# Transposing q and k by the DMA crossbar instead of TensorE in a linear-attention and MLP kernel

## The chip, the cores and the metric

The kernel runs on one core of a Trainium2 chip. The metric is the device time of one execution in microseconds (us). "Before" took 228.87 us as the median of three runs (227.82 to 230.3) when the prediction was written. The profile shows one such execution, whose span of instructions was 227.0 us. TensorE (PE) had its full clock throughout (0.999).

## The reference, cut to what matters

There are two parts. The first is causal linear attention with a decay for each head, in blocks, over q, k and v of shape (4, 8, 768, 64). Its output, as 3072 rows of 512 columns, goes through a two-layer MLP of width 2048 with a smooth ReLU.

```python
for b in range(nb):                                   # blocks of the sequence
    intra = einsum('bhic,bhjc->bhij', qb, kb) * Dmask # scores
    intra = einsum('bhij,bhjd->bhid', intra, vb)
    inter = einsum('bhid,bhde->bhie', qb * lam_pow, kv_state)
    out[:, :, sl] = intra + inter
    kv_state = lam_block * kv_state + einsum('bhsd,bhse->bhde', kb_dec, vb)
h = x @ w_in
g = where(h >= 1, h, where(h <= -1, 0, (h + 1) ** 2 / 4))
out = g @ w_out
```

## The kernel before: the parts that matter

The rows are cut into 24 chunks of 128 (`NCH`). The scores need q and k with the head dimension on the partitions, so each chunk's k and q (both 128 x 512) are transposed: first cast to bf16 by ScalarE, then transposed by eight TensorE instructions into PSUM (the memory that TensorE's results go to here), then copied or scaled from there by VectorE into SBUF (the on-chip memory that holds the other tiles).

```python
def f_t(c):                                           # TensorE
    ptt[c] = pp_t.tile([128, 2, HP, 128], BF16, name="pt", tag="pt")
    for i, x in ((1, ks), (0, qs)):
        for hp in range(HP):                          # HP = 4
            nc.tensor.transpose(out=ptt[c][:, i, hp, :], in_=pair(x[c], hp), identity=ident)

def f_kb(c, hi):                                      # VectorE: k, block-diagonal
    ...
        nc.vector.tensor_copy(kbd[c % NKB][HD[hi], :, :, hi, :], ptt[c][HD[hi], 1].rearrange(...))

def f_qT(c):                                          # VectorE: q times the decay table
    nc.vector.tensor_tensor(qT[c], ptt[c][:, 0], tab_q[:, c % NCB], op=AX.mult)

def f_vb(c, g, hi):                                   # v, block-diagonal, by DMA; VP = 12
    (nc.gpsimd if c < VP else nc.sync).dma_start(out=o, in_=i)
```

The MLP's first layer (`f_l1`, PSUM tile `ph`), its activation (r on ScalarE; t, w and gT on VectorE) and its second layer (`f_l2`, PSUM tile `py`) run between the attention's pieces.

The order of instructions on each engine is fixed when the kernel is built. A small planner in the kernel (`run_plan`) has a booked duration, a landing time and a due time for each operation, plays them through, and writes each engine's program in the order that it found. `STEP` spaces the due times. Each engine then works through its program in that order, so a wrong booked time can cost real time.

## Time and profile before

| engine | busy before | what it does |
|---|---|---|
| PE | 96% of the span | the MLP, the scores, the transposes |
| VectorE (DVE) | 70% | t, w, gT; kbd, qT and masks of the attention |
| ScalarE (ACT) | 60% | r, the casts, copies out of PSUM |
| GpSimd (POOL) | 33% | scaling of v, issue of some DMAs |

A share of busy time says little about what an engine's work is worth. That is read from the chain of waits (what ended last, followed back) and from the busy time of single stretches. The prediction below quotes those lines. One more is from the view of waits of the kernel before, with columns of total us, number of waits and the longest:

```profile
ACT r L347 <- DVE w L357: 9.7, 8, 1.2
```

ScalarE waits for VectorE's w step, because w is what frees the buffers that r is written to.

### The profile page before, as it was taken

What the parts mean: (1) busy time and instruction counts of PE and PEld (TensorE: products, weight loads), DVE (VectorE), ACT (ScalarE), POOL (GpSimd) and SP (SyncE); (2) the same over time, 40 slices, a digit from 0 to 9 for tenths busy, and PEclk for the clock granted to TensorE, in tenths of its full rate; (3) what the DMA queues carried; (4) which work ended last, traced back from release to release, by engine and by line L of the source; (5) the groups of instructions that cost most, each with busy time, mean ns of one, the idle gap of its engine ahead of it and who ended that gap; (6) DMA issues with size and microseconds to landing.
All of it is one profiled execution on the core that took longest, in us unless ns stands there. A gap on an engine that the chain in (4) does not pass through costs nothing.

```text
span 227.0 us, 5657 instructions
## 1 busy us (share of the span) xinstructions
PE 217.0 (96%) x2272; PEld 158.7 (70%) x2308; DVE 159.5 (70%) x276; ACT 136.6 (60%) x249; POOL 74.0 (33%) x95
## 2 busy tenths in 40 slices
PE   7799999989999999999999999999999999999993
PEld 2467888867787778877877777776777776766441
DVE  6635889998689998996678687783875775544300
ACT  6768575844988667588547648645565554545121
POOL 8999765956899420221032210000000000000000
PEclk9999999999999999999999999999999999999999
DMA  5999998969999999497687732112101101110212
GB/s 147 232 255 212 268 204 220 201 144 275 269 253 272 243 271 238 76 241 155 163 194 149 198 88 70 37 35 69 48 3 46 49 0 49 48 46 3 92 46 92
DMA packets 78570, 32.36 MB, mean 143 GB/s; under 512 B 69648, under 2 KB 73744, under 8 KB 78544
## 3 DMA queue, kind: packets, MB, share of 16 engines
q1 hardware_dynamic: 71632, 21.77, 38.8%
q0 software_dynamic: 6768, 10.23, 20.5%
q8 instruction: 18, 0.29, 0.5%
q14 instruction: 8, 0.07, 0.1%
q10 hardware_dynamic: 144, 0.00, 0.0%
HBM read 27.27 MB, written 6.29 MB: 148 GB/s over the span
## 4 chain that ended last, share of the span: by engine, by line
PE 78%; DVE 12%; POOL 4%; DMA 3%; issue 1%; ACT 0%; POOLq 0%; ACTq 0%
PE ph L339 32%; PE py L378 32%; PE pt L267 4%; DVE gT L372 3%; DMA w_in_sb<-in_moe_w_in_dram 3%; PE ps L298 3%; DVE t L353 3%; PE po L322 2%; DVE w L357 2%; PE po L316 2%; PE pu L286 2%; DVE sc L309 1%; POOL x2f L420 1%; DVE kbd L273 1%; POOL vn L254 1%
## 5 line engine op out<-in xcount | busy, mean ns | idle before, releaser
L347 ACT ACTIVATE r<-ph,one 128x512 bf16<-128x512 f32 x96 | 65.8, 687 | 60.5 <-PE ph L339 42.2
L339 PE MATMUL ph<-xT,w_in_sb 128*128 128x128 bf16 (+1 forms) x1152 | 98.9, 237 | 0.2 <-DMA w_in_sb<-in_moe_w_in_dram 0.2
L339 PEld LDWEIGHTS <-w_in_sb 128*128 128x128 bf16 x1152 | 81.7, 98 | 15.5 <-DMA w_in_sb<-in_moe_w_in_dram 0.4
L378 PE MATMUL py<-w_out_sb,gT 128*128 128x512 bf16 x351 | 89.8, 379 | 1.7
L378 PEld LDWEIGHTS <-gT 128*128 128x128 bf16 x384 | 34.6, 98 | 27.5
L254 POOL TENSOR_TENSOR vn<-x2f,tab_k 128x512 bf16<-128x512 f32 x24 | 27.6, 1151 | 52.2 <-DMA vi<-vn 22.7
L353 DVE TENSOR_SCALAR t<-r 128x1024 bf16<-128x1024 bf16 x48 | 25.3, 526 | 23.8 <-ACT r L347 23.7
L372 DVE TENSOR_TENSOR gT<-w,t 128x1024 bf16<-128x1024 bf16 x48 | 37.3, 778 | 1.1
L357 DVE TENSOR_TENSOR w<-r,t 128x1024 bf16<-128x1024 bf16 x48 | 35.4, 738 | 1.4
L309 DVE TENSOR_TENSOR sc<-ps,causal 128x512 bf16<-128x512 f32 (+1 forms) x40 | 22.1, 553 | 7.4 <-PE ps L298 7.4
L383 ACT COPY osb<-py 128x512 f32<-128x512 f32 x24 | 14.0, 585 | 15.7 <-PE py L378 15.2
L273 DVE COPY kbd<-pt 64x512 bf16<-64x512 bf16 x40 | 16.8, 419 | 7.1 <-PE pt L267 6.7
L261 POOL DMA_DIRECT2D vi<-vn x32 | 20.2, 647 | 2.7 <-POOL vn L254 2.4
L280 DVE TENSOR_TENSOR qT<-pt,tab_q 128x512 bf16<-128x512 bf16 x24 | 16.6, 690 | 1.7 <-ACT kbd L271 1.1
L329 ACT CAST xT<-po 128x512 bf16<-128x512 f32 x24 | 14.0, 583 | 5.6 <-PE po L322 4.1
L290 ACT CAST ubd<-pu 64x256 bf16<-64x256 f32 x40 | 14.6, 365 | 2.4 <-PE pu L286 2.1
L248 ACT CAST qs<-x0f 128x512 bf16<-128x512 f32 x23 | 14.2, 618 | 0.7 <-DMA x0f<-in_q_dram 0.7
L298 PE MATMUL ps<-qT,kbd 128*128 128x128 bf16 (+1 forms) x160 | 13.3, 206 | 1.4 <-DVE qT L280 0.8
L248 ACT CAST ks<-x1f 128x512 bf16<-128x512 f32 x23 | 14.2, 616 | 0.1
L316 PE MATMUL po<-qT,ubd 128*128 128x128 bf16 x80 | 13.8, 221 | 0.0
L298 PEld LDWEIGHTS <-kbd 128*128 128x128 bf16 x160 | 10.5, 98 | 4.4 <-issue 1.5
L322 PE MATMUL po<-sc,vi 128*128 128x128 bf16 (+1 forms) x160 | 13.2, 206 | 0.1
(50 smaller groups left out, 136.2 us busy)
## 6 DMA issues: line engine op xcount, KB each, us to landing
out_dram<-osb SPq DMA_DIRECT2D x24, 256.0 KB, 2.0
x1f<-in_k_dram SPq DMA_DIRECT2D x18, 256.0 KB, 4.1
x0f<-in_q_dram SPq DMA_DIRECT2D x18, 256.0 KB, 4.3
x2f<-in_v_dram SPq DMA_DIRECT2D x17, 256.0 KB, 4.1
w_in_sb<-in_moe_w_in_dram POOLq DMA_DIRECT2D x4, 512.0 KB, 7.5
w_out_sb<-in_moe_w_out_dram POOLq DMA_DIRECT2D x4, 512.0 KB, 9.8
x2f<-in_v_dram POOLq DMA_DIRECT2D x7, 256.0 KB, 4.7
x1f<-in_k_dram POOLq DMA_DIRECT2D x6, 256.0 KB, 6.6
```

Of the source, the lines that this page charges most:

```text
L248: nc.scalar.copy(out=t, in_=qkv_ld[c, x])
L254: nc.gpsimd.tensor_tensor(vn[c % NV].rearrange("p a b d -> p (a b) d"), qkv_ld[c, 2], _bc(tab_k[:, c % NCB, :], 2, D), op=AX.mult)
L261: (nc.gpsimd if c < VP else nc.sync).dma_start(out=o, in_=i)
L273: nc.vector.tensor_copy(kbd[c % NKB][HD[hi], :, :, hi, :], ptt[c][HD[hi], 1].rearrange("p a (b d) -> p a b d", b=2))
L298: nc.tensor.matmul(pst[c, g][:, hp, :], lhsT=kbd[c % NKB][:, hp, g].rearrange("p a d -> p (a d)"), rhs=qT[c][:, hp, 64 * g:], start=True, ...
L309: nc.vector.tensor_tensor(sc_sb[c][g], pst[c, g], _bc(causal[:, 0:128 - 64 * g], 1, HP), op=AX.mult)
L339: nc.tensor.matmul(ph[:, j * m:(j + 1) * m], lhsT=w_in_sb[:, ko, (i + j) * 128:(i + j + 1) * 128], rhs=xT[s][:, ko, p * m:(p + 1) * m], st ...
L347: nc.scalar.activation(out=r_t[grp][:, i, :], in_=ph_t[s, ni, part], func=AF.Relu, bias=one[:, 0:1])
L353: nc.vector.tensor_scalar(t_t[grp], r_t[grp], 0.5, 1.0, op0=AX.mult, op1=AX.min)
L357: nc.vector.tensor_tensor(w_t[grp], r_t[grp], t_t[grp], op=AX.subtract)
L372: nc.vector.tensor_tensor(o, w, t, op=AX.mult)
L378: nc.tensor.matmul(py_t[s, ms], lhsT=gT[s][:, ko, ms * 128:(ms + 1) * 128], rhs=w_out_sb[:, ko, :], start=(ko == 0), stop=(ko == FO - 1))
```

## The change

The intent is to take 128 transposes (16 chunks of eight) off TensorE. Chunks 8 to 23 are transposed by the DMA crossbar (a DMA that transposes while it copies), SBUF to SBUF, in one instruction for q and k together. It is issued by SyncE (SP), which here only issues DMAs. The other edits make room for it: q and k share one tile with four buffers, the v copies of chunks 12 to 23 move from SP to GpSimd, loads are released 30 us ahead of need, due times are spaced closer, and some of the planner's booked times change (left out below).

```diff
+    NQK, NXT, XT = 4, 2, 8
+    qkp = ctx.enter_context(tc.tile_pool(name="qkp", bufs=NQK))
+    xtp = ctx.enter_context(tc.tile_pool(name="xtp", bufs=NXT))
...
+    def f_xt(c):
+        t = xtp.tile([128, 2, HP, 128], BF16, name="xq", tag="xq")
+        ptt[c] = t
+        nc.sync.dma_start_transpose(out=t.rearrange("p a h k -> p (a h) k"), in_=qk[c].rearrange("p a h d -> p (a h d)"))
...
-    VP = 12
+    VP = 24
...
-                    rel = u.own - AHEAD if u.key[0] == "t" and u.key[1] >= CPS else 0
+                    rel = o_due(u.key[1]) - (14000 if u.key[0] == "t" else 18000) if u.key[0] in ("t", "xt") and u.key[1] >= CPS else o_due(u.key[1]) - 30000 if u.key[0] == "li" and u.key[1] > SW else 0
...
-    T0, STEP, LEAD = 24000, 1047, 3000
+    T0, STEP, LEAD = 24000, 1015, 3000
...
+        if c < XT:
+            add(t, "PE", mm(*[128] * 8), lambda c=c: f_t(c), need, due=od - 9000, extra=FILL)
+        else:
+            add(t, "SP", 2000, lambda c=c: f_xt(c), need, due=-0.7, extra=4500)
```

`f_kb` and `f_qT` are the same instructions as before, but for these chunks they read the transposed data from SBUF (xq) and no longer from PSUM (pt).

## The prediction

> **What bounds the kernel now.** I read the page's first part and its chain first, then the busy time in stretches, then the chain in order of time in two of them, and last the groups that the change touches.
>
> ```profile
> PE 217.0 (96%) x2272; PEld 158.7 (70%) x2308; DVE 159.5 (70%) x276; ACT 136.6 (60%) x249; POOL 74.0 (33%) x95
> ...
> PE 78%; DVE 12%; POOL 4%; DMA 3%; issue 1%; ACT 0%; POOLq 0%; ACTq 0%
> ```
>
> TensorE (PE) is busy for 96% of the span and holds 78% of the chain of waits. VectorE (DVE) holds 12% of the chain, so somewhere it is the bound for a while. A share over the whole span hides where, so next come the stretches; their columns are the stretch, its length, then busy time of PE, PEld, DVE, ACT and POOL.
>
> ```profile
> 60.00:80.00 20.00, 19.47 (x276) 16.13 (x279) 19.08 (x28) 16.05 (x33) 15.37 (x20) 1.00 1.09 256
> 80.00:100.00 20.00, 19.49 (x266) 15.69 (x268) 18.82 (x35) 14.23 (x26) 4.04 (x3) 1.00 0.87 204
> 120.00:140.00 20.00, 19.84 (x180) 14.54 (x183) 15.24 (x28) 13.21 (x26) 3.50 (x3) 1.00 0.53 129
> 160.00:180.00 20.00, 19.84 (x184) 14.45 (x184) 14.33 (x28) 12.34 (x21) 0.00 (x0) 1.00 0.11 41
> ```
>
> From 100 us on PE is busy for 19.8 of 20 us, VectorE for about 14, and the DMA engines have little to do (0.53 of their time, then 0.11). Between 60 and 100 us VectorE is nearly full too, and GpSimd (POOL) is busy for 15.4 of 20 us at first. A busy PE may still be a PE that runs with gaps, so I look at the chain in order of time in the late stretch; the columns are start, length, and what.
>
> ```profile
> 158.26 0.86 PE py L378 x4
> 159.13 0.87 PE ph L339 x8
> 160.00 0.45 PE pt L267 x8
> 160.45 0.86 PE py L378 x4
> 161.31 0.87 PE ph L339 x8
> 162.18 0.05 issue
> 162.24 0.81 PE py L378 x3
> ```
>
> Each piece starts where the one before ends; in the part from 156 to 178 us "issue", the only piece that isn't matmul work, is 0.7%. So the eight transposes of a chunk, four of k and four of q, cost the full 0.45 us of their issue there: PE work removed is time removed, as long as nothing takes its place. The other kind of stretch reads like this:
>
> ```profile
> 67.83 0.69 DVE sc L309
> 68.52 1.98 DVE t L353
> ...
> 75.42 0.61 DVE w L357
> 76.05 1.42 DVE gT L372
> ```
>
> From 67.8 to 85 us the chain runs on VectorE without a break, and the t step, whose shortest record is 408 ns, takes 1.98 us here. Last, the groups concerned:
>
> ```profile
> L267 PE MATMUL pt<-ident,ks 128*128 128x128 bf16 x96 | 9.3, 219 | 0.0
> L273 DVE COPY kbd<-pt 64x512 bf16<-64x512 bf16 x40 | 16.8, 419 | 7.1 <-PE pt L267 6.7
> L280 DVE TENSOR_TENSOR qT<-pt,tab_q 128x512 bf16<-128x512 bf16 x24 | 16.6, 690 | 1.7 <-ACT kbd L271 1.1
> L353 DVE TENSOR_SCALAR t<-r x48: 408/426/2051, 20.6 to 210.2; 128x1024 bf16<-128x1024 bf16 x48
> L261 SPq DMA_DIRECT2D vi<-vn x48: 590/597/1339, 89.0 to 156.3; - x48
> ```
>
> The first line's busy 9.3 us is not the cost to count: its 219 ns overlap with each other, and eight transposes advance the chain by 0.45 us, 56 ns each.
>
> **What the Trainium skill says.** (1) "VectorE: DVE Perf Modes", The perf-mode tier table: a copy from bf16 SBUF may run 4x, one with a PSUM operand at most 2x; a tensor_tensor with an fp32 operand stays 1x. The trace agrees on the ends it shows: 128x1024 bf16 SBUF to SBUF in 408 ns, the PSUM copy of 512 columns in 419 ns. (2) "SBUF — State Buffer", Who interferes with whom: VectorE in a two-port mode and GpSimd take an exclusive lock on a shared port pair, and a VectorE instruction with two SBUF inputs contends with a GpSimd instruction that reads SBUF. The trace agrees: t goes from 408 to 2051 ns, and averages 1.03 us (4.14 us for 4) in the stretch from 60 to 80 us where GpSimd is busy for 77%. (3) "DMA: Bandwidth & Descriptors", Latency and other measured facts, gives an effective 261 GB/s for a DMA transpose, and its part on the DMA transpose says that it must be issued from SP or ACT and must land in SBUF; no run here shows its speed yet. (4) "Advanced Engine Details and Errata", X-Bar Transpose (TRN2): transposes on two queues at once corrupt each other; here all sixteen are issued from SP, so no extra wait is needed.
>
> **The change, part by part.**
>
> PE work removed. Chunks 8 to 23 are 16 of 24, so 16 x 0.45 = 7.2 us of PE issue go. The stretches put the transposes of chunks 8 to 10 between 60 and 80 us; in the chain I count 14 of the 16 at full length, and two (chunks 9 and 10) fall in the VectorE stretch from 67.8 to 85 us. So 14 x 0.45 = 6.3 us are on the path that sets the end, and 0.9 us lie beside VectorE work.
>
> VectorE work removed. The 32 kbd copies of these chunks now read bf16 from SBUF. An estimate from the t step: it has 1024 columns in 408 ns; 512 columns fewer at four per cycle of 0.96 GHz (that page's clock) are 133 ns less, so 275 ns against 419, and the diff's own plan has 260. That is 0.15 x 32 = 4.8 us less VectorE work, of which some 0.6 us lies in the VectorE stretch (four copies). The qT multiply has an fp32 table as its second operand, so it stays at 690 ns.
>
> VectorE work added. The vi copies of chunks 12 to 23 go from the SP queue to GpSimd's (VP 12 to 24): 12 x 4 = 48 at 647 ns (the mean of that group on POOL) = 31 us of GpSimd time. With the 1.15 us v scaling that makes 3.74 us per chunk of about 8 us, or 45% of GpSimd. Both kinds then block t, the new kbd copies, and (by the scaling's reads) w, gT and qT. At 77% GpSimd load a group of t, w and gT lost about 0.6 + 0 + 0.37 = 1.0 us (1.03 against 0.41, and 1.06 against 0.69); at 45% I estimate 0.5 us, 2.5 us per 20 us. VectorE then stands at about 14.3 - 0.8 + 2.5 = 16 of 20 us, still below PE. Some of these delays come at a bad moment: ScalarE waits for "w" to free its r buffers for 9.7 us in 8 waits already, at most 1.2 us each. I charge 1.0 us.
>
> DMA and the queue. Per chunk 128 x 1024 bf16 = 256 KiB cross the crossbar; at the page's 261 GB/s an estimate of 1.0 us, 16 us in all, over a stretch in which the engines stand at 0.53 and then 0.11. The plan in the diff books 2.0 us of SP issue and 4.5 us to landing. SP loses 48 x 0.6 = 29 us of vi issue and gains 16 x 2.0 = 32 us: level. The loads are released 30 us ahead of need rather than as early as buffers allow, so the load peak and the burst of GpSimd work around 60 to 80 us spread out; that should return part of the PE time lost in the VectorE stretch, 0.5 us with the cheaper copies. In-order SP behind a store that waits for its output tile (37.4 us of such waits after 85 us) can make a transpose late: I charge 0.4 us.
>
> STEP falls from 1047 to 1015 ns over 192 steps, 6.1 us: it is a priority for the planned order and no work, but it says that the planner expects about that much.
>
> Sum: 6.3 + 0.5 - 1.0 - 0.4 = 5.4 us of gain in the middle; since two of the transposes in the VectorE stretch may also come back (0.9) and the charges are the least certain terms, I take 6.4. So 228.87 - 6.4 = 222.5 us, a span near 220.6.
>
> **The rivals.** First, the transpose is late: transpose after cast, landing, copy, scores is a longer way than PE to PSUM, and only two xq buffers hold it. A chunk has some 8 us, and the plan has 2.0 + 4.5 us plus 2.5 of slack; if landing takes 8 us and more, PE stands still in front of each chunk's scores. One us lost per chunk makes 16 us and a slower kernel, near 238. Against it: loads of the same 256 KB land in 4.1 us beside a full DMA, and the constants look measured. Second, GpSimd's blocking makes VectorE the bound to the end of the attention: at 19 of 20 us from 60 to 80 us PE still got 19.47, so even that costs about 0.4 us per 20 us, 2 to 3 us in all: 224 to 225. Third, the transposes were hidden anyway: then nothing moves, 228 to 229. The unbroken chain of PE speaks against it.
>
> **Range and chances.** The clean case (all 7.2 us and a little from VectorE) is 221; the second rival lies at 225; the first has a long tail. Range 219.8 to 226.5. The 2% line is 224.3 us, 1.8 us above my number: faster 0.70, within 2% 0.24, slower 0.06.
>
> **What would show it.** Right: eight-transpose pieces gone from the chain after 60 us, PE still at 19.8 of 20 us from 100 us on, kbd copies of 64x512 near 275 ns, qT at 690, GpSimd near 105 us busy with 80 vi issues, t longer than 426 ns on average after 100 us, SP issue near 2 us per transpose, landing under 6 us. Wrong: PE idle put down to the xq transfer, or to qT or kbd ahead of the scores; ScalarE's waits for "w" grown well past 10 us; a VectorE chain that goes on beyond 100 us; a transpose that takes SP or the DMA engines far longer than a load.

## The result, and the profile after

The changed kernel took 222.49 us as the median of four runs (220.14 to 222.97), against 228.81 us before (227.82 to 230.3). The ratio is 0.9698, with a 95% interval of 0.9609 to 0.9787. A ratio is the mean time of one kernel's fast runs over that of the other's of the same rounds, so it is not quite the ratio of these medians. The prediction was 222.5 us.

First the page's busy times and the chain of the changed kernel:

```profile
PE 210.5 (96%) x2147; PEld 152.2 (69%) x2180; DVE 154.8 (70%) x276; ACT 136.2 (62%) x249; POOL 103.7 (47%) x143
...
PE 81%; DVE 8%; POOL 5%; DMA 4%; issue 1%; ACT 0%; POOLq 0%; ACTq 0%
```

PE is 6.5 us less busy (217.0 to 210.5) and still busy for 96% of a shorter span. VectorE's share of the chain fell from 12% to 8%. GpSimd is busy for 103.7 us where it was 74.0. The same stretches as in the prediction follow, and the one from 100 to 120 us (length, then busy time of PE, PEld, DVE, ACT and POOL; the last three columns are the PE clock, the DMA share and GB/s):

```profile
60.00:80.00 20.00, 19.79 (x236) 14.87 (x239) 17.68 (x29) 16.05 (x30) 15.47 (x21) 1.00 1.08 235
80.00:100.00 20.00, 19.73 (x278) 16.14 (x279) 16.25 (x29) 13.97 (x28) 11.34 (x16) 1.00 1.03 227
100.00:120.00 20.00, 19.84 (x236) 15.58 (x238) 19.10 (x35) 14.87 (x28) 10.78 (x16) 1.00 0.92 195
120.00:140.00 20.00, 19.79 (x179) 14.58 (x182) 16.02 (x31) 12.98 (x25) 10.03 (x14) 1.00 0.86 201
160.00:180.00 20.00, 19.84 (x181) 14.41 (x182) 14.75 (x28) 11.89 (x21) 3.60 (x5) 1.00 0.22 56
```

Late on, PE is as full as before, and in the two later stretches VectorE, with GpSimd working beside it, stands at 16.0 and 14.8 of 20 us. Between 60 and 100 us VectorE is less full than it was (17.68 and 16.25 against 19.08 and 18.82), but from 100 to 120 us it is fuller, 19.10 against 14.80, so its full stretch has partly moved. PE is still busy for 19.84 us there, and no VectorE step of that stretch is on the chain. The chain in order of time shows the late stretch without transposes:

```profile
156.74 0.86 PE py L386 x4
157.60 0.22 PE pu L294 x4
157.83 0.22 PE ps L306 x4
158.05 0.87 PE ph L347 x8
158.92 0.05 issue
158.97 0.81 PE py L386 x3
```

Scores (ps) and MLP pieces follow one another, and no piece of eight transposes stands between them. The VectorE stretch on the chain is shorter. It ran from 67.8 to 85 us. Now it begins where this fence does and ends at 94.6 us:

```profile
87.18 0.44 DVE t L361
87.64 1.41 DVE w L365
...
92.92 0.35 DVE t L361
93.29 0.69 DVE w L365
```

Last, what the new tile costs, from the view of the tile xq:

```profile
L281 DVE COPY kbd<-xq x32: 273/291/470, 72.0 to 176.2; 64x512 bf16<-64x512 bf16 x32
L259 SPq DMA_TRANSPOSE xq<-qk x16: 1237/1305/3252, 64.2 to 166.2; - x16
L288 DVE TENSOR_TENSOR qT<-xq,tab_q x16: 681/693/898, 72.8 to 177.3; 128x512 bf16<-128x512 bf16 x16
...
DMA to landing us min/median/max: 2.7/4.1/6.2
```

The three numbers before the comma are the shortest, median and longest in ns. At the median a copy out of xq takes 291 ns (from PSUM the mean was 419), the multiply is unchanged at 693, a transpose occupies SP for 1.3 us (3.3 us at most), and it lands 4.1 us after its issue. The same view lists nobody who waited for a transpose.

Where in the run was the time won? I compared when the two traces reach the same point of the MLP, which has the same sequence of blocks in both. The 65th weight load of the first layer starts at 24.31 us before and at 25.40 us after, so the changed kernel is 1.09 us late at this point. The 353rd weight load of the second layer starts at 216.02 and at 209.23 us, so there it is 6.78 us early. In this pair of profiles the middle therefore gained 7.87 us, and the start gave 1.09 back.

The start depends on when the first weights land. In the twelve later profiles of kernels of this family that same weight load starts anywhere from 24.6 to 26.8 us, although GpSimd's first instructions, which issue these loads, were in the same order in the profiles where I compared them. In the six profiles after, e0, e4, e5, e8 and e9 below, whose kernels took about the same time, the stretch between the two marks took 183.80 to 184.38 us, while its start lay between 24.93 and 26.73 us; so most of what these profiles differ in is the start. There is only one profile of the kernel before (24.31 us), so I can't tell whether its start is earlier in general.

### The profile page after: what moved, and what is told of

Read it like the earlier page. It is cut to its first block, busy times and chain, and to the rows that moved or that the text cites. A ratio compares the mean times of both kernels' runs of the same rounds, so it can differ in the third digit from the quotient of the medians.

```text
span 220.2 us, 5365 instructions
## 1 busy us (share of the span) xinstructions
PE 210.5 (96%) x2147; PEld 152.2 (69%) x2180; DVE 154.8 (70%) x276; ACT 136.2 (62%) x249; POOL 103.7 (47%) x143
## 4 chain that ended last, share of the span: by engine, by line
PE 81%; DVE 8%; POOL 5%; DMA 4%; issue 1%; ACT 0%; POOLq 0%; ACTq 0%
PE py L386 35%; PE ph L347 34%; DMA w_in_sb<-in_moe_w_in_dram 4%; PE ps L306 3%; PE po L330 3%; DVE w L365 2%; PE po L324 2%; PE pu L294 2%; DVE gT L380 2%; DVE t L361 2%; POOL x2f L428 1%; POOL vn L262 1%; PE pt L275 1%; DVE sc L317 1%; POOL x1f L428 1%
## 5 line engine op out<-in xcount | busy, mean ns | idle before, releaser
L347 PEld LDWEIGHTS <-w_in_sb 128*128 128x128 bf16 x1152 | 80.5, 98 | 12.4 <-DMA w_in_sb<-in_moe_w_in_dram 1.3
L386 PEld LDWEIGHTS <-gT 128*128 128x128 bf16 x384 | 35.8, 98 | 28.7
L269 POOL DMA_DIRECT2D vi<-vn x80 | 50.2, 644 | 10.2 <-POOL vn L262 6.2
L361 DVE TENSOR_SCALAR t<-r 128x1024 bf16<-128x1024 bf16 x48 | 27.5, 572 | 28.6 <-ACT r L355 28.6
L365 DVE TENSOR_TENSOR w<-r,t 128x1024 bf16<-128x1024 bf16 x48 | 36.9, 769 | 1.2
L380 DVE TENSOR_TENSOR gT<-w,t 128x1024 bf16<-128x1024 bf16 x48 | 35.3, 735 | 0.9
L252 ACT CAST qk<-x0f 128x512 bf16<-128x512 f32 x23 | 14.1, 615 | 0.7 <-DMA x0f<-in_q_dram 0.6
L252 ACT CAST qk<-x1f 128x512 bf16<-128x512 f32 x23 | 14.1, 613 | 0.0
L229 PE MATMUL py<-idle 128*128 128x512 bf16 x33 | 10.8, 464 | 1.5 <-DVE one L117 1.2
L330 PEld LDWEIGHTS <-vi 128*128 128x128 bf16 x160 | 11.1, 98 | 1.4
```

The lines of the kernel that those rows point to most:

```text
L252: nc.scalar.copy(out=t, in_=qkv_ld[c, x])
L330: nc.tensor.matmul(po[:, hp, 64 * g:], lhsT=vi[c % NV][:, hp, g].rearrange("p a d -> p (a d)"), rhs=sc_sb[c][g][:, hp, :], start=(cb == 0 ...
L347: nc.tensor.matmul(ph[:, j * m:(j + 1) * m], lhsT=w_in_sb[:, ko, (i + j) * 128:(i + j + 1) * 128], rhs=xT[s][:, ko, p * m:(p + 1) * m], st ...
L361: nc.vector.tensor_scalar(t_t[grp], r_t[grp], 0.5, 1.0, op0=AX.mult, op1=AX.min)
L365: nc.vector.tensor_tensor(w_t[grp], r_t[grp], t_t[grp], op=AX.subtract)
L380: nc.vector.tensor_tensor(o, w, t, op=AX.mult)
```

## The experiments

Twelve kernels ran, in three groups on one chip each. Every one gave the correct result. The table has them in the order of the text.

| run | edit to the changed kernel | median us | ratio to before, 95% |
|---|---|---|---|
| e0_after | none | 221.99 | 0.9721 (0.9671 to 0.9770) |
| e1_dummy | TensorE transposes put back, unused | 228.63 | 1.0021 (0.9959 to 1.0083) |
| e2_rest | no chunk through the crossbar | 230.38 | 1.0087 (1.0047 to 1.0127) |
| e3_xt16 | chunks 16 to 23 only | 225.99 | 0.9839 (0.9800 to 0.9878) |
| e4_vp12 | v copies back on SP | 222.61 | 0.9758 (0.9712 to 0.9804) |
| e5_nopace | loads as early as possible | 222.67 | 0.9712 (0.9677 to 0.9748) |
| e8_step1047 | STEP 1047 | 222.02 | 0.9670 (0.9630 to 0.9711) |
| e7_nxt1 | one xq buffer | 249.35 | 1.0862 (1.0812 to 1.0912) |
| e9_nxt1_plan | one xq buffer, planner told measured times | 222.20 | 0.9683 (0.9638 to 0.9727) |
| e6_xt5 | chunks 5 to 23 | 220.56 | 0.9645 (0.9599 to 0.9692) |
| e10_xt5_nxt3 | chunks 5 to 23, three xq buffers | 221.73 | 0.9664 (0.9621 to 0.9707) |
| e11_xt4_nxt3 | chunks 4 to 23, three xq buffers | 227.32 | 0.9902 (0.9863 to 0.9942) |

Before took 229.09, 229.37 and 229.53 us (medians of eleven runs) in the three groups. The medians are over all runs of a kernel, a few slow among them. The groups are e0, e1, e2, e4; then e3, e5, e6, e7; then e8 to e11.

### Is the gain TensorE's issue time?

Theory A says that the gain is the 0.45 us per chunk that PE no longer spends. Rival B says that the transposes were mostly hidden, and that the cheaper VectorE copies and the spread loads brought the gain.

The changed kernel as it stands is the mark.

> The changed kernel once more, on the chip that runs the next three: 222.5 us by every theory; it is the mark that they are compared with.

It gave 221.99 us.

The second run puts PE's work back and leaves all else. The eight transposes of each chunk are issued again, beside the crossbar's, into a PSUM tile that nobody reads. A comparison of the two programs showed that the order of every other engine's instructions stayed as it was.

```diff
-        nc.sync.dma_start_transpose(out=t.rearrange(...), in_=qk[c].rearrange(...))
+        nc.sync.dma_start_transpose(out=t.rearrange(...), in_=qk[c].rearrange(...)); f_t(c, pp_t.tile([128, 2, HP, 128], BF16, name="pt", tag="pt"))
```

(Left out: `f_t` takes the tile to write as a second argument in this run.)

> The changed kernel with the eight TensorE transposes of each of chunks 8 to 23 put back beside the crossbar transpose, their result read by nobody; every other engine's order stays as it is. Theory A (the gain is TensorE issue time taken off the path): 16 x 0.45 = 7.2 us come back, 229 to 230 us. Rival B (the gain comes from the cheaper VectorE copies and the spread loads, and the transposes were mostly hidden): at most 1.5 us come back, under 224 us.

It took 228.63 us, and the ratio went from 0.9721 to 1.0021: 0.0300 x 229.09 = 6.9 us came back, uncertain by some 1.8 us. Within this that is the whole gain of e0_after (6.4 us), and it agrees with the 7.2 us of theory A. Rival B had at most 1.5 us and falls. By the two marks used above the middle took 190.42 us, 6.35 us more than in e0_after's profile (184.07 us). Its chain in order of time shows the pieces again, each at full length:

```profile
158.08 0.86 PE py L386 x4
158.95 0.45 PE pt L275 x8
159.39 0.87 PE ph L347 x8
```

The third run is the opposite half: all of the change but the crossbar.

```diff
-    NQK, NXT, XT = 4, 2, 8
+    NQK, NXT, XT = 4, 2, 24
-    T0, STEP, LEAD = 24000, 1015, 3000
+    T0, STEP, LEAD = 24000, 1047, 3000
```

> Everything of the change but the crossbar: all 24 chunks transposed on TensorE again, with the new pacing of the loads, four q/k buffers, and all vi copies on GpSimd (STEP back at 1047, which fits the TensorE work). Theory A: no gain without the crossbar, 228 to 230 us. Rival B: the pacing alone brings 2 us or more, 227 us or less. If GpSimd's blocking costs what I charged, 1 us, this kernel shows it as 229.5 to 230 us.

It took 230.38 us, 0.9% more than before (0.5 to 1.3%). So the rest brings no gain by itself. On its chain, VectorE has a second stretch, from 105.9 to 114.4 us, which the kernel before has not:

```profile
105.95 0.42 DVE kbd L281
...
111.81 2.23 DVE gT L380
```

A gT step takes 2.23 us here, where 0.69 is the undisturbed one. GpSimd was at work during most of it: it issued v copies up to 112.4 us and then scaled v until 113.5 us, so being held up by GpSimd fits. But this stretch can't be named as what cost the 0.9%. By the two marks the middle of this profile took 190.95 us, no more than the 191.70 us before; it is late at the first mark already (26.80 us against 24.31), after a stretch from 16 to 20 us in which the granted clock was 0.57. What cost the 0.9% is open.

The fourth sends only half of the chunks through the crossbar.

```diff
-    NQK, NXT, XT = 4, 2, 8
+    NQK, NXT, XT = 4, 2, 16
```

> Only chunks 16 to 23 through the crossbar (8 of 24), all else as in the changed kernel. Theory A (0.45 us of TensorE issue a chunk): half the gain, 8 x 0.45 = 3.6 us, so 222.3 + 3.6 = 225.9 us, plus up to 1.3 us if the rest of the change costs what it costs without the crossbar. Rival C (the gain comes from relief in the crowded middle, 60 to 115 us, so chunks 8 to 15 hold nearly all of it): 228 us or more.

225.99 us against an expected 225.9. The chunks 16 to 23, where only PE is full, bring their share. So the gain isn't a matter of the crowded middle, and rival C falls.

### Do the parts around it matter?

The v copies of chunks 12 to 23 back on the SP queue:

```diff
-    VP = 24
+    VP = 12
```

> The changed kernel with the vi copies of chunks 12 to 23 left on the SP queue, where they were before. If GpSimd's blocking of VectorE costs 1 us on the path, as I charged: 221 to 222 us. If it is hidden: 222.5 us. If the SP queue, which would carry 48 copies of 0.6 us and 16 transposes of 1.3 us, makes transposes or loads late: 224 us or more.

222.61 us, ratio 0.9758 against 0.9721 with overlapping intervals; the middle took 183.92 us by the marks, against 184.07. GpSimd's work fell (in the stretch from 80 to 100 us from 10.98 to 3.48 us busy), and nothing was won. So the charge of 1 us that I had put on GpSimd's blocking isn't seen on the path; a part of it that the busier SP queue gave back can't be excluded. Nor does the SP queue overflow: it carries both kinds of work, and its trace shows nobody waiting for a transpose.

Loads as early as their buffers allow:

```diff
- ... else o_due(u.key[1]) - 30000 if u.key[0] == "li" and u.key[1] > SW else 0
+ ... else 0
```

> The changed kernel with the loads of chunks 8 to 23 released as early as their buffers allow, as before, and not 30 us ahead of need. I gave the pacing a part of 0.5 us. If it relieves the stretch from 60 to 100 us: 222.8 to 223.5 us. If it does nothing: 222.3 us. If transposes behind a crowd of loads come late: 224 us or more.

222.67 us, ratio 0.9712. The pacing does nothing to the time that these runs could see.

The old spacing of the due times:

```diff
-    T0, STEP, LEAD = 24000, 1015, 3000
+    T0, STEP, LEAD = 24000, 1047, 3000
```

> The changed kernel with STEP back at 1047, so the plan's due times lie up to 6 us behind what TensorE can do. If STEP is only a priority: 222.3 us, within 1 us. If the loads and transposes, released against those due times, now come late: 224 us or more, near the 6.1 us by which the due times move.

222.02 us. STEP is a priority and no work, as the prediction had it.

### How much room does the transpose have?

My first rival in the prediction was a late transpose. One buffer for xq in place of two forces the next transpose to wait until the last has been copied out:

```diff
-    NQK, NXT, XT = 4, 2, 8
+    NQK, NXT, XT = 4, 1, 8
```

> The changed kernel with one xq buffer in place of two, so a transpose can start only when the chunk before has been copied out of it. My first rival in the prediction held that the two buffers and the way through the crossbar leave little room: then TensorE stands still before each chunk's scores, 2 us or more in all, 224.5 us or more. If the way has room (issue to landing 4.1 us, copies about 1.3 us, a chunk every 8 us): within 1 us of 222.3 us.

It took 249.35 us, 27 us more, far past what I had expected of either theory. It looks like proof that one buffer is too few for the crossbar. The trace says otherwise. The SP queue's own timeline shows the transpose issued as soon as the qT multiply before it had ended at 154.2 us:

```profile
154.17 1.24 SPq L259 DMA_TRANSPOSE xq<-qk  x1
...
163.03 1.29 SPq L259 DMA_TRANSPOSE xq<-qk  x1
```

In this stretch a transpose lands 2.8 us after issue, so this one was there at 157.0 us. VectorE's timeline has the copies out of xq at

```profile
160.74 0.58 DVE L281 COPY kbd<-xq 64x512 bf16<-64x512 bf16 x2
161.35 0.69 DVE L288 TENSOR_TENSOR qT<-xq,tab_q 128x512 bf16<-128x512 bf16 x1
```

which is 3.7 us after the landing. VectorE wasn't held by the transfer. Its program had put other steps before the copy, since the planner books 2.0 us of issue, 4.5 us more to the landing and 2.5 us of slack for the queue. With one buffer those booked times follow one another for each chunk. The next run keeps the single buffer and corrects the booked times.

```diff
-    NQK, NXT, XT = 4, 2, 8
+    NQK, NXT, XT = 4, 1, 8
-            add(t, "SP", 2000, lambda c=c: f_xt(c), need, due=-0.7, extra=4500)
+            add(t, "SP", 1300, lambda c=c: f_xt(c), need, due=-0.7, extra=2000)
-                    lat = ... DSLACK if u.eng == "SP" else LAT
+                    lat = ... DSLACK if u.eng == "SP" and u.key[0] != "xt" else LAT
```

> One xq buffer again, but with the plan that fixes each engine's order told what the last run measured of a transpose: 1.3 us of issue and 3.3 us from issue to landing, without the 2.5 us of slack for the queue (it had been told 2.0, 6.5 and 2.5). Theory E (the 27 us of the one-buffer run come from the order that a pessimistic plan fixed, since the copies out of xq stood 3.7 us behind the landing): most of it comes back, 222 to 226 us. Rival F (one buffer is too few for the crossbar's real latency): 240 us or more.

222.20 us: all 27 us came back, with one buffer. The SP queue issues a transpose every 8.1 us, the pace of the chunks:

```profile
118.44 1.29 SPq L259 DMA_TRANSPOSE xq<-qk  x1
...
126.50 1.30 SPq L259 DMA_TRANSPOSE xq<-qk  x1
```

So the second buffer of the change makes room for the planner's booking, not for the crossbar.

### Does more of it help?

Three more chunks, whose transposes fall where the DMA engines are full:

```diff
-    NQK, NXT, XT = 4, 2, 8
+    NQK, NXT, XT = 4, 2, 5
```

> The crossbar for chunks 5 to 23 as well (three more). Theory A: another 3 x 0.45 = 1.35 us, 221 us. Rival D (between 30 and 60 us the DMA engines are full and the SP queue stands behind the wait for the last weight load, so a transpose is late and TensorE waits for it): 222.5 us or more, with TensorE idle put down to qT or kbd ahead of the scores.

220.56 us, the lowest median of all, and five of its six runs lie at 222.25 us or below. The ratio of 0.9645 is below e0_after's 0.9721, but the intervals overlap (up to 0.9692, and from 0.9671), and the two ran in different groups. Within the third group, the same chunks with a third buffer (e10_xt5_nxt3, below) come to 0.9664, where chunks 8 to 23 come to 0.9670 (e8_step1047). So a gain of the size that 3 x 0.45 = 1.35 us promises is neither shown nor excluded. Rival D was half right. The profiled run, at 223.08 us the slowest of the six, lost time where a transpose was late. The first fence is from its chain between 80 and 102 us; the columns of the second, from its view of waits there, are total, number and longest:

```profile
82.03 10.74 DMA xq<-qk x2
```

```profile
DVE kbd L281 <- DMA xq<-qk: 2.2, 2, 1.9
PE ps L306 <- DVE sc L317: 1.8, 1, 1.8
```

A third xq buffer, so that such a transpose can start earlier:

```diff
-    NQK, NXT, XT = 4, 2, 8
+    NQK, NXT, XT = 4, 3, 5
```

> Crossbar for chunks 5 to 23 with three xq buffers in place of two. The run with two lost about 2 us in its profile where a transpose landed late behind loads; if the third buffer lets it start earlier: 219.5 to 220.5 us. If the full DMA engines set the landing, not the buffer: 220.6 us, as with two.

221.73 us, ratio 0.9664: no better than with two. The median landing is 5.2 us in both. In this profile VectorE waited only 0.7 us for a transpose, and the middle took 181.69 us by the marks, against 184.90 in e6_xt5's and 183.80 to 184.38 with chunks 8 to 23. So where hardly a transpose is late, more of them win some 2 us in the middle; over all runs the times don't show it.

One chunk more still, with q/k buffers to match:

```diff
-    NQK, NXT, XT = 4, 2, 8
+    NQK, NXT, XT = 5, 3, 4
```

> Crossbar for chunks 4 to 23, three xq buffers and five q/k buffers. By TensorE issue alone 4 x 0.45 = 1.8 us less than the changed kernel: 220 to 220.5 us. If the DMA engines, full between 20 and 60 us, make the transposes of chunk 4 and 5 late: 222 us or more.

227.32 us: most of the gain is gone. Two stretches of this run show where (columns as above); then follow one line of its waits between 20 and 110 us, the landing line of its tile xq, and two pieces of its chain:

```profile
40.00:50.00 10.00, 5.84 (x54) 3.48 (x52) 5.08 (x10) 4.22 (x7) 7.70 (x10) 1.00 1.17 189
50.00:60.00 10.00, 9.54 (x91) 6.63 (x91) 5.07 (x11) 5.68 (x10) 4.96 (x8) 0.83 1.03 243
```

```profile
DVE kbd L281 <- DMA xq<-qk: 4.9, 2, 2.7
```

```profile
DMA to landing us min/median/max: 2.7/4.6/12.2
```

```profile
25.18 15.70 DMA x1f<-in_k_dram
...
43.30 7.70 DMA w_out_sb<-in_moe_w_out_dram
```

Between 40 and 50 us PE is busy for 5.84 of 10 us, and in the next 10 us its granted clock is 0.83. (All six runs have a mean clock of 0.983 to 0.992.) The DMA engines are full there (a share over 1), one transpose takes 12.2 us to land, and VectorE waits for xq for 4.9 us. That looks like the first rival of the prediction. But the chain doesn't go through xq there: it goes through a load of k that landed after 15.70 us and the last weights of the second layer, which GpSimd issued behind it and which landed at 51.0 us. So several transfers were late together. Whether the late transposes, the loads beside them, the order in the SP queue or the buffers cost the time was not tried.

## Why the prediction was right, by its own steps

**The bound.** Right. PE was the bound, and its chain was without gaps. Putting the work back (e1_dummy) brought the time back.

**PE work removed.** 6.3 us on the path, and perhaps 0.9 more. Measured by e1_dummy against e0_after: 6.9 us, but the two intervals are 0.6% and 0.5% wide either way, together some 1.8 us, so this can't tell 6.3 from 7.2. The middle of the two profiles differs by 6.35 us.

**VectorE work removed.** Estimated 275 ns a copy, measured 291; 690 ns for the multiply, measured 693. I gave this and the spread loads 0.5 us together; the pacing's part is nothing that e5_nopace could see. The VectorE stretch on the chain shrank from 17 to 7.4 us.

**GpSimd's blocking.** Charged 1.0 us; this is the term that was most wrong. GpSimd's busy time came out as said (103.7 against 105 us). But I expected 0.5 us more for each group of t, w and gT, 2.5 us more VectorE time per 20 us. Over the instructions that start between 100 and 180 us, such a group took 1.96 us on average, against 1.88 before: 0.09 us more. It is t alone that grew, from 0.43 to 0.55 us, as the prediction's signs had it. In the whole run the page's groups have t, w and gT at 25.3 + 35.4 + 37.3 = 98.0 us before and 27.5 + 36.9 + 35.3 = 99.7 us after. The scaling by GpSimd's busy share, from a stretch where it worked without pause, was not a good one. ScalarE's wait for w, whose growth well past 10 us would have been a sign of error, is no longer in the list at all. And in e4_vp12 taking the copies off GpSimd won nothing.

**DMA and SP.** I took 2.0 us of issue from the plan; the median is 1.3 us. Landing was said to be under 6 us; the median is 4.1, the longest 6.2, and nobody waited. The charge of 0.4 us for a late transpose isn't seen in the changed kernel.

**The sum.** The terms added up to 5.4 us, and I chose 6.4 because the charges were the least certain. The medians differ by 6.3 us. So the number is right partly because two things offset each other: in the pair of profiles the middle gained more than I had (7.87 us, with charges that didn't fall due), and the start was 1.09 us late, which no term foresaw.

**The rivals.** The late transpose wasn't there in this change, but it exists: e6_xt5's chain has 10.74 us of it. GpSimd making VectorE the bound didn't happen with the crossbar: even where VectorE was busy for 19.10 of 20 us, PE was busy for 19.84. The hidden transposes are refuted by e1_dummy.

## What to carry to other kernels

When one engine's chain has no gaps, count the issue time of what you take off it (0.45 us for eight overlapping transposes, not eight times 219 ns), and check that the way that replaces it has slack where it runs: here nobody waited for a transpose, even in stretches where the DMA engines were full (shares of 1.08 and 1.03), but with three or four chunks more VectorE did wait. To test such a claim, put the removed work back with its result unused; that isolates it better than undoing the change. If the program's order comes from a planner, a slow variant may show the planner's booked times and not the hardware: correct them before you blame the hardware, as the 27 us of the one-buffer run show.

## What the Trainium skill lacked or had wrong

- "VectorE: DVE Perf Modes", The three transpose paths, lists 1309 ns for one 128x128 block through the DMA crossbar. Eight such blocks in one instruction landed in 2.7 us at the quickest and 4.1 us in the median here, so the figure is not to be multiplied by the blocks. SP was occupied for 1.24 us at least in this profile.
- "DMA: Bandwidth & Descriptors", Latency and other measured facts: from its 261 GB/s I estimated 1.0 us of transfer for 256 KiB. (The page gives that figure for a non-contiguous middle dimension, and 350 to 400 GB/s for the contiguous case, which I left out.) No page that I read says how long a crossbar transpose takes from issue to landing beside other traffic; the runs show 2.7 us with little traffic and up to 12.2 us with the DMA engines full.
- "SBUF — State Buffer", Who interferes with whom, states the lock between VectorE and GpSimd, and the traces agree with it for single steps (a gT of 2.23 us against 0.69, beside GpSimd's scaling of v). It doesn't say what it costs on the whole: with 29.7 us more of GpSimd work (74.0 to 103.7), t, w and gT together took 1.7 us more.
